# Attention output of two head pairs in the score tiles, fill steps behind AV, and two more GEMM blocks in the AV banks

## The chip, the cores and the metric

The kernel runs on one core of a Trainium2 chip. The metric is the device time of one execution in microseconds (us); smaller is better. The median of three runs of the kernel before is 334.15 us (333.97 to 334.6). Engines: PE multiplies matrices into PSUM, ACT does activations, DVE does vector work, POOL does elementwise work that doesn't touch PSUM, and SP issues DMAs.

## The reference, cut to what matters

```python
scores = scale * np.matmul(q, k.transpose(0, 1, 3, 2))     # 8 batches, 8 heads, 576 tokens, 64 wide
decay = cum[:, :, :, None] - cum[:, :, None, :]            # cum: running sum of log f
attn = softmax(np.where(causal, -1e9, scores + decay))
x = np.matmul(attn, v)                  # -> (4608 tokens, 512)
h = x @ w_in                            # 512 -> 2048
g = 0.5 * h * (1.0 + erf(h / sqrt(2)))  # gelu
out = g @ w_out                         # 2048 -> 512
```

The decay is put into the values: each key's row of V is multiplied by its weight, and a 65th column holds the weight itself, so that AV (attention weights times V) gives both the sum and its divisor.

## The kernel before, in words

The program goes through the eight batches one by one; the order of every engine's work is written out by hand, and each engine takes its instructions in that order. Heads are worked in four pairs, 0 to 3. Batches 0 and 1 have code of their own; `attention(b)` is for batches 2 to 7, and the change is in what it does for batches 3 to 7. Such a batch has two stages.

*Attention.* For each pair and each of four score tiles, `scores` (L299) multiplies K with Q into a score tile, ACT takes exp of it (L329), POOL masks the diagonal (L331). Between the score tiles PE does steps of the second GEMM of the batch before, taken from a generator (`take`, L590; `gemm2_rows`, L489). A step is one or two matmuls of 512 columns (L509); there are 64, in four groups of 16 by rows of tokens. 53 of them lie between score tiles (`FILL`). Then comes AV: `attend` (L343) does 15 matmuls of 65 columns for each head (L350), and `normalize` (L358) on DVE takes the reciprocal of five divisors (L363) and multiplies 128x320 values by them into `x` (L364). When both heads of a pair are done, `x_dma` (L388) has SP issue a transposing DMA of `x` into slice i of `xT`. Ten of the last eleven steps of the fill are put among the AV groups by `FILL_AV` (L826): none before pair 0, then three, two and two before pairs 1 to 3, and one between the two heads of each of these. A copy of a partial sum that was put off (L887) and the last step follow; that step's sum goes out by L533 and L537.

*First GEMM and gelu.* `gemm1` (L400) does blocks of 128 of the 2048 columns: four matmuls of 512 columns (L405), one for each contraction slice, and slice i is what pair i's transpose brings. `gemm1_open` (L829) opens seven blocks: all slice 0 of blocks 0 to 5, then all slice 1, and so on, so that later slices may come later. Blocks 0 to 3 lie in the two score tiles, 4 and 5 in the two AV banks, 6 in another bank. The other blocks (L981 on) follow one by one. ACT takes gelu of each (L425) and then its bank is free. Meanwhile DVE puts the next batch's Q and K in order (`untangle`, L269) and POOL weighs its V (`weigh_v`, L288).

PSUM has eight banks: `s_psum`, two score tiles of two banks each; `o_psum`, two single banks for AV; `m_psum`, two single banks for the GEMMs. A pool hands its buffers out in turn, and whoever writes one first waits until its last reader is through. Blocks 7 and 10 to 15 take `m_psum`; blocks 8 and 9 take `o_psum` (`spare`, L416), by the line

```python
aside = ffb in ((7, 8) if b == 2 else (8, 9)) if b > 1 else b == 1 and ffb % 4 < 2
```

After block 15 the next batch's attention begins, and the first two groups of its fill take `o_psum` and then `m_psum` (`PLAN`, L472). After batch 7 the second GEMM of batch 7 and both GEMMs of the 64 last tokens of all batches follow (L435).

Of the kernel before, what the change touches and what calls it, by code (L numbers as in the profile page):

```python
# [9 lines left out]
FP32 = mybir.dt.float32  # L10
BF16 = mybir.dt.bfloat16
Act = mybir.ActivationFunctionType
Alu = mybir.AluOpType
PSUM = bass.MemoryType.PSUM

P = 128
S = 576
D = 64
H = 8
HP = 4  # L20
NBLK = 5
# [20 lines left out]
def where(n, m):  # L42

    q = K0[m]
    for t, parts in enumerate(STILES):
        c = 0
        for nn, q0, w in parts:
            if nn == n and q0 <= q and q + P <= q0 + w:
                return t, c + q - q0
            c += w  # L50
    raise KeyError((n, m))
# [3 lines left out]
def kernel(  # L55
# [10 lines left out]
    nc = tc.nc  # L66
# [20 lines left out]
    x_pool = ctx.enter_context(tc.tile_pool(name="x", bufs=4))  # L87
# [3 lines left out]
    s_psum = ctx.enter_context(tc.tile_pool(name="s_psum", bufs=2, space=PSUM))  # L91
# [37 lines left out]
    def load_v(b, h0=0, h1=H, eng=nc.sync, ns=range(NBLK)):  # L129
        if b >= B:  # L130
            return
        for n in ns:
            p0 = D if n == NBLK - 1 else 0
            eng.dma_start(
                v_sb[p0:P, h0:h1, n, :],
                v[b, h0:h1, K0[n] + p0 : K0[n] + P].rearrange("h p d -> p h d"),
            )
# [203 lines left out]
    o_of, x_of, xT_of = {}, {}, {}  # L341

    def attend(b, i, h, ms, pool=o_psum, tag="o"):  # L343
        if (b, i, h) not in o_of:
            o_of[b, i, h] = pool.tile([P, NBLK, D + 1], FP32, tag=tag, name="o")
        o = o_of[b, i, h]
        for m in ms:
            for n in range(m + 1):
                t, c = where(n, m)
                nc.tensor.matmul(  # L350
                    o[:, m, :],
                    e_of[b, i, t][:, h, c : c + P],
                    vw_of[b][:, 2 * i + h, n, :],
                    start=(n == 0),
                    stop=(n == m),
                )

    def normalize(b, i, h):  # L358
        if (b, i) not in x_of:
            x_of[b, i] = x_pool.tile([P, NBLK, 2, D], BF16, tag="x", name="x")  # L360
        o = o_of[b, i, h]
        r = x_pool.tile([P, NBLK], FP32, tag="r", name="r")
        nc.vector.reciprocal(r, o[:, :, D])  # L363
        nc.vector.tensor_tensor(  # L364
            x_of[b, i][:, :, h, :],
            o[:, :, 0:D],
            r.unsqueeze(2).to_broadcast([P, NBLK, D]),
            Alu.mult,
        )

    def xT(b):
        if b not in xT_of:
            xT_of[b] = xT_pool.tile([P, n_dm, XC], BF16, tag="xT", name="xT")
        return xT_of[b]
# [13 lines left out]
    def x_dma(b, i):  # L388
        nc.sync.dma_start_transpose(
            xT(b)[:, i, :].rearrange("d (m p) -> d m p", p=P),  # L390
            x_of[b, i].rearrange("p m h d -> p (m h d)"),
        )

    def x_tail(b):
        nc.gpsimd.tensor_copy(tails[:, :, b * TL : (b + 1) * TL], xT(b)[:, :, XC - TL :])
# [20 lines left out]
    def spare():  # L416
        return o_psum.tile([P, TC], FP32, tag="o", name="ps1")
# [167 lines left out]
    def gemm2_third():  # L585
        yield from gemm2_second(0)
        yield from gemm2_rows(0, PLAN_0)
        yield from gemm2_rows(1, PLAN_1)

    def take(gen, n):  # L590
        for _ in range(n):
            if next(gen, "end") == "end":
                return
# [229 lines left out]


    FILL = [[8, 4, 3, 3], [3, 3, 3, 3], [3, 3, 3, 3], [3, 3, 3, 2]]
    FILL_AV = [(0, 0), (3, 1), (2, 1), (2, 1)]  # L826
    FILL_2 = [[8, 8, 8, 8], [8, 8, 4, 4], [4, 4, 4, 4], [4, 4, 4, 4]]

    def gemm1_open(b):  # L829


        pss = []
        for _ in range(2):
            wide = s_psum.tile([P, 2, 512], FP32, tag="s", name="ps1")
            pss += [wide[:, 0, :], wide[:, 1, :]]
        pss += [spare(), spare(), m_psum.tile([P, TC], FP32, tag="m", name="ps1")]
        for kt in range(2):
            for ffb in range(6):
                gemm1(b, ffb, (kt,), pss[ffb])
        gemm1(b, 6, (0, 1), pss[6])  # L840
        for ffb in range(7):
            gemm1(b, ffb, (2,), pss[ffb])
        for pair in ((4,), (5,), (6,), (0, 1), (2, 3)):
            for ffb in pair:
                gemm1(b, ffb, (3,), pss[ffb], False)
            for ffb in pair:
                gelu(b, ffb, pss[ffb])

    def attention(b):


        fill = gemm2_third() if b == 2 else gemm2_rows(b - 1, PLAN)
        counts = FILL_2 if b == 2 else FILL

        def av(i, n=0):
            for h in range(2):
                attend(b, i, h, (0, 1, 2, 3, 4))
                normalize(b, i, h)
                if h == 0:
                    take(fill, n)  # L860
            x_dma(b, i)

        for i in range(HP):
            for t in range(4):
                scores(b, i, t)
                take(fill, counts[i][t])
                if t == 1 and b == 2 and i > 0:
                    av(i - 1)
                    if i == 1:
                        load_v(3)  # L870
                if b == 2 and (i, t) == (0, 3):
                    weigh_v(b, 2)
                    weigh_v(b, 3)
                if b > 2 and i == 0 and t == 1:
                    load_v(b + 1)
                if b > 2 and t == 0 and i < 2:
                    transpose_dma(b + 1, 4 * i, 4 * i + 4)
                if b == 2 and t == 1 and i == 1:
                    transpose_dma(3, 0, 4)
        if b == 2:  # L880
            take(fill, 4)
            av(HP - 1)
        else:
            for i, (n0, n1) in enumerate(FILL_AV):
                take(fill, n0)
                av(i, n1)
            put_off.pop()()  # L887
        if b == 2:
            take(fill, 4)
            transpose_dma(3, 4, 8)  # L890
        take(fill, 999)

        if b == 2:
            pss = [gemm1(b, ffb, (0, 1)) for ffb in range(2)]
            pss += [spare(), spare()]
            for ffb in range(2):
                gemm1(b, ffb, (2,), pss[ffb])
            for ffb in (2, 3):
                gemm1(b, ffb, (0, 1, 2), pss[ffb])
            for ffb in range(4):  # L900
                gemm1(b, ffb, (3,), pss[ffb])
            more = s_psum.tile([P, 2, 512], FP32, tag="s", name="ps1")
            gemm1(b, 4, ps=more[:, 0, :])
        else:
            gemm1_open(b)
        if b + 1 < B:
            untangle(b + 1, 0)
            weigh_v(b + 1, 0)
        x_tail(b)
# [64 lines left out]
    for b in range(B):  # L974
        if b == 0:
            first_attention()
        elif b == 1:
            second_attention()
        else:
            attention(b)  # L980
        for ffb in range(4 if b < 2 else 5, n_ff):  # L981
            if b == 0 and ffb in HELD:
                continue
            aside = ffb in ((7, 8) if b == 2 else (8, 9)) if b > 1 else b == 1 and ffb % 4 < 2
            if b <= 2 or ffb > 6:
                gemm1(b, ffb, ps=spare() if aside else None)
            if b == 1 and ffb % 2 == 0:
                at = HELD[(ffb - 4) // 2]
                gelu(0, at, h_of[at])
            if b == 0:  # L990
                if ffb == 4:
                    attend_tail()
                if ffb == 5:
                    tail_0()
                if ffb == 7:
                    weigh_v(1, 0)
                    load_w_out(0)
                    weigh_v(1, 1)
                    load_w_out(1)
                    load_qk_tokens(2)  # L1000
                if ffb == 8:
                    transposes_first(1, 0, o_psum, "o")
            elif b + 1 < B:
                first, gap = (5, 3) if b == 1 else (1, 4)
                at, late = divmod(ffb - first, gap)
                if late == 0:
                    untangle(b + 1, at)
                if late == gap - 2 and (b > 1 or at < 2):
                    weigh_v(b + 1, at)
                if ffb == (9 if b == 1 else 14):  # L1010
                    load_qk_tokens(b + 2)
# [34 lines left out]
```

## Time and profile before

| what | value |
|---|---|
| median of three runs | 334.15 us |
| profiled execution | 335.06 us, its span 333.4 us |
| PE busy | 323.6 us, 97% of the span |
| ACT, DVE, POOL busy | 203.1, 189.1, 134.1 us |
| first GEMM, L405 (512 matmuls on `xT`) | 115.1 us busy, 1.7 us idle before them |
| AV, L350 (840 matmuls) | 33.9 us busy |
| division, L364 (56) and L363 (56) | 27.5 and 10.7 us busy, 491 and 192 ns each |
| transposes of `x`, issued by SP | 24, median 2.5 us from issue to landing, 4.8 at most |
| instruction queue's packets in the DMA records | 26 of 16 KB |

The profile is of one execution. The page gives each engine's busy time, the chain of work that ended last, and the costliest groups of instructions with what their engine waited for. The timeline gives start (us from the span's beginning), duration, engine, line, operation, output and input, count, and in brackets the idle time before it and what ended it. Consecutive matmuls overlap in it, because a matmul's row runs to the end of its pipeline: the time that one adds is the distance between starts. Batches 3 to 7 begin their AV at 126.8, 161.9, 197.2, 231.9 and 266.5 us and their first GEMM at 133.0, 168.1, 203.6, 238.2 and 272.7 us.

### The profile page before, as it was taken

How to read it: one execution, taken by the hardware profiler on the slowest of the kernel's cores; microseconds unless marked ns; L12 is line 12 of the kernel's file. 1: busy time of each engine (PE TensorE's matmuls, PEld its weight loads, DVE VectorE, ACT ScalarE, POOL GpSimd, SP SyncE). 2: the span in 40 equal slices, each digit the busy share in tenths (PEclk: the TensorE clock that was granted, in tenths of full speed). 3: DMA queues.
4: the chain of work that ended last, by engine and by line, in shares of the span. 5: the costliest groups of instructions: out<-in, count | busy, mean ns of one | idle time of the engine just before them, and what ended most of it. 6: DMA issues, size and time to landing. Idle time of an engine off the chain costs nothing.

```text
span 333.4 us, 8154 instructions
## 1 busy us (share of the span) xinstructions
PE 323.6 (97%) x3327; PEld 173.6 (52%) x3327; DVE 189.1 (57%) x432; ACT 203.1 (61%) x296; POOL 134.1 (40%) x260
## 2 busy tenths in 40 slices
PE   8999999999999999999999999999999999999995
PEld 4664455445544467445644565456645564444443
DVE  5852756754649637993599459964896370010011
ACT  4986786965526894389618980899078916405600
POOL 8997873057336152725345443535152500000000
PEclk9999999999999999999999999999999999999999
DMA  7999999959999697399978987779600151020022
GB/s 120 195 199 213 198 194 147 216 113 219 185 196 179 113 222 146 71 144 190 211 93 119 175 206 135 105 136 218 155 21 2 65 101 43 2 90 36 0 53 76
DMA packets 94949, 44.19 MB, mean 133 GB/s; under 512 B 74176, under 2 KB 89792, under 8 KB 94912
## 3 DMA queue, kind: packets, MB, share of 16 engines
q1 hardware_dynamic: 77760, 27.16, 40.7%
q0 software_dynamic: 16752, 15.99, 30.3%
q8 instruction: 26, 0.43, 0.6%
q10 hardware_dynamic: 400, 0.52, 0.4%
q14 instruction: 11, 0.09, 0.1%
HBM read 36.85 MB, written 9.44 MB: 139 GB/s over the span
## 4 chain that ended last, share of the span: by engine, by line
PE 82%; DMA 11%; POOL 5%; issue 1%; ACT 0%; DVE 0%; POOLq 0%
PE ps L405 33%; PE ps L509 26%; PE ps L449 8%; PE o L350 6%; PE s L319 6%; DMA xT<-x 5%; DMA q<-in_k_dram 3%; DMA k<-in_k_dram 3%; POOL v_sb L169 2%; PE ps L573 1%; POOL q L120 1%; PE ps L549 1%; POOL k L120 1%; POOL w_in_sb L184 1%; POOL vw L288 0%
## 5 line engine op out<-in xcount | busy, mean ns | idle before, releaser
L425 ACT ACTIVATE g<-ps 128x512 bf16<-128x512 f32 x138 | 75.8, 618 | 89.4 <-PE ps L405 88.3
L405 PE MATMUL ps<-xT,w_in_sb 128*128 128x512 bf16 x512 | 115.1, 379 | 1.7 <-DMA xT<-x 1.6
L509 PE MATMUL ps<-w_out_sb,g 64*128 64x512 bf16 (+1 forms) x751 | 111.2, 376 | 0.0
L329 ACT ACTIVATE e<-s 128x896 bf16<-128x896 f32 x112 | 87.8, 836 | 14.9 <-PE s L319 12.7
L405 PEld LDWEIGHTS <-w_in_sb 128*128 128x128 bf16 x576 | 55.2, 97 | 68.8 <-issue 6.2
L331 POOL TENSOR_SCALAR_AFFINE_SELECT e<-e 128x256 bf16<-128x256 bf16 (+1 forms) x135 | 49.1, 383 | 76.1 <-ACT e L329 75.7
L509 PEld LDWEIGHTS <-g 64*128 64x128 bf16 (+1 forms) x751 | 41.9, 94 | 27.4 <-issue 1.3
L288 POOL TENSOR_TENSOR vw<-v_sb,wT 128x640 bf16<-128x640 f32 (+1 forms) x30 | 38.2, 1276 | 38.0 <-PE o L350 23.0
L269 DVE COPY qT<-tq 64x288 bf16<-64x288 bf16 x96 | 41.8, 436 | 3.1 <-DMA tq<-q 1.6
L269 DVE COPY kT<-tk 64x288 bf16<-64x288 bf16 x96 | 40.7, 424 | 2.7 <-DMA tk<-k 1.1
L523 DVE COPY ot<-ps 128x512 f32<-128x512 f32 x20 | 13.8, 692 | 49.5 <-PE ps L509 49.5
L319 PE MATMUL s<-qT,kT 64*128 64x256 bf16 (+1 forms) x336 | 37.8, 275 | 0.8 <-DVE kT L241 0.6
L350 PEld LDWEIGHTS <-e 128*128 128x128 bf16 x840 | 31.5, 98 | 9.1 <-issue 6.1
L350 PE MATMUL o<-vw,e 128*128 128x65 bf16 x840 | 33.9, 194 | 0.0
L458 DVE COPY ot<-ps 128x512 f32<-128x512 f32 (+2 forms) x9 | 5.7, 632 | 49.2 <-PE ps L449 49.2
L364 DVE TENSOR_TENSOR x<-o,r 128x320 bf16<-128x320 f32 x56 | 27.5, 491 | 1.9
L319 PEld LDWEIGHTS <-kT 64*128 64x128 bf16 x336 | 18.1, 94 | 19.8 <-issue 3.5
L449 PE MATMUL ps<-w_out_sb,g 128*128 128x512 bf16 (+2 forms) x144 | 28.0, 355 | 0.0
L449 PEld LDWEIGHTS <-g 128*128 128x128 bf16 x144 | 13.5, 98 | 14.5
L533 DVE TENSOR_TENSOR ot<-ot,ps 128x512 f32<-128x512 f32 x27 | 18.6, 688 | 2.5
L363 DVE RECIPROCAL r<-o 128x5 f32<-128x5 f32 x56 | 10.7, 192 | 7.8 <-PE o L350 7.8
L405 PE MATMUL ps<-tails,w_in_sb 128*128 128x512 bf16 x64 | 14.3, 378 | 0.0
(90 smaller groups left out, 186.2 us busy)
## 6 DMA issues: line engine op xcount, KB each, us to landing
out_dram<-ot SPq DMA_DIRECT2D x32, 256.0 KB, 2.5
v_sb<-in_v_dram SPq DMA_DIRECT2D x24, 256.0 KB, 4.8
q<-in_q_dram POOLq DMA_DIRECT2D x6, 576.0 KB, 6.2
k<-in_k_dram POOLq DMA_DIRECT2D x6, 576.0 KB, 8.4
v_sb<-in_v_dram POOLq DMA_DIRECT2D x17, 128.0 KB, 6.1
w_in_sb<-in_moe_w_in_dram POOLq DMA_DIRECT2D x4, 512.0 KB, 8.2
w_out_sb<-in_moe_w_out_dram POOLq DMA_DIRECT2D x4, 512.0 KB, 7.6
v_sb<-in_v_dram SPq DMA_DIRECT2D x6, 128.0 KB, 4.5
```

The costliest lines, as they stand in the source:

```text
L269: nc.vector.tensor_copy(rows[:, odd], src[odd * D : (odd + 1) * D, 2 * i + h].rearrange("d j p -> d p j"),)
L288: eng.tensor_tensor(vw(b)[:, hs, n0:n1, 0:D], v_sb[:, hs, n0:n1, :], w.unsqueeze(3).to_broadcast([P, 2, n1 - n0, D]), Alu.mult,)
L319: nc.tensor.matmul(to, *ab, start=half < 0, stop=half == 1 or not masked)
L329: nc.scalar.activation(et[:, :, z:c], st[:, :, z:c], Act.Exp, scale=scale)
L331: nc.gpsimd.affine_select(out=et[:, :, c0 + z : c0 + P], in_=et[:, :, c0 + z : c0 + P], compare_op=Alu.is_ge, fill=0.0, base=z, pattern=[[ ...
L350: nc.tensor.matmul(o[:, m, :], e_of[b, i, t][:, h, c : c + P], vw_of[b][:, 2 * i + h, n, :], start=(n == 0), stop=(n == m),)
L364: nc.vector.tensor_tensor(x_of[b, i][:, :, h, :], o[:, :, 0:D], r.unsqueeze(2).to_broadcast([P, NBLK, D]), Alu.mult,)
L405: nc.tensor.matmul(ps, w_in_sb[:, kt, ffb * P : (ffb + 1) * P], src[:, kt, 0:TC], start=(kt == 0), stop=(kt == n_dm - 1),)
L425: nc.scalar.activation(g_of[c][ffb], ps, Act.Gelu)
L449: nc.tensor.matmul(pss[ts][:, c0:c1], g_of[c][kt][:, ts * P : (ts + 1) * P], w_out_sb[:, kt, c0:c1], start=(kt == 0), stop=(kt == n_ff - 1),)
L509: nc.tensor.matmul(banks[r], g_of[c][kt][rows, ts * P : (ts + 1) * P], w_out_sb[rows, kt, :], start=kt == (steps.index("r") if r else 0), ...
L533: nc.vector.tensor_tensor(ot, ot, bank, Alu.add)
```

## The change

In batches 3 to 7 the AV of pairs 1 and 2 goes into two score tiles, one bank for each head, in place of the AV banks; each of these pairs is divided by one reciprocal of 10 divisors and one multiplication of 128x640 values for both heads. Pairs 0 and 3 stay in the AV banks with a division for each head. All eleven last steps of the fill come behind the AV of all pairs. In the first GEMM blocks 12 and 13 take the AV banks too.

```diff
-    FILL_AV = [(0, 0), (3, 1), (2, 1), (2, 1)]
...
+    def av_both(b, i):
+        st = s_psum.tile([P, 2, 512], FP32, tag="s", name="o2")
+        both = st[:, :, 0 : NBLK * (D + 1)].rearrange("p h (m d) -> p h m d", m=NBLK)
+        for h in range(2):
+            o_of[b, i, h] = both[:, h]
+            attend(b, i, h, (0, 1, 2, 3, 4))
+        x_of[b, i] = x_pool.tile([P, NBLK, 2, D], BF16, tag="x", name="x")
+        r = x_pool.tile([P, 2, NBLK], FP32, tag="r2", name="r2")
+        nc.vector.reciprocal(r, both[:, :, :, D])
+        nc.vector.tensor_tensor(
+            x_of[b, i].rearrange("p m h d -> p h m d"),
+            both[:, :, :, 0:D],
+            r.unsqueeze(3).to_broadcast([P, 2, NBLK, D]),
+            Alu.mult,
+        )
+        x_dma(b, i)
...
         else:
-            for i, (n0, n1) in enumerate(FILL_AV):
-                take(fill, n0)
-                av(i, n1)
+            av(0)
+            av_both(b, 1)
+            av_both(b, 2)
+            av(3)
             put_off.pop()()
...
-            aside = ffb in ((7, 8) if b == 2 else (8, 9)) if b > 1 else b == 1 and ffb % 4 < 2
+            aside = ffb in ((7, 8) if b == 2 else (8, 9, 12, 13)) if b > 1 else b == 1 and ffb % 4 < 2
```

In the changed kernel the wide reciprocal is L838, the wide multiplication L839 and the put-off copy L906.

## The prediction

> **What bounds the kernel now.** I read the page first. TensorE is busy for 97% of the span, every slice grants it full clock, and by the page's chain of waits most of the span is PE work. The change leaves PE's instructions as they are, so all it can win is PE time lost inside batches 3 to 7. The view of waits gives the sum that PE's own row admits to:
>
> ```profile
> PE 323.6 (97%) x3327; PEld 173.6 (52%) x3327; DVE 189.1 (57%) x432; ACT 203.1 (61%) x296; POOL 134.1 (40%) x260
> ...
> q8 instruction: 26, 0.43, 0.6%
> ```
> ```profile
> PE ps L405 <- DMA xT<-x: 1.6, 3, 0.6
> ```
>
> Three waits, 1.6 us, all of the first GEMM (L405) for transposed attention output. A modelled matmul end hides part of a wait, so I take distances between starts. The timeline of PE in batch 4, from the first pair's AV on (start, duration, engine, line, operation, tiles, count):
>
> ```profile
> 161.94 1.13 PE L350 MATMUL o<-vw,e 128*128 128x65 bf16 x30
> 162.90 0.81 PE L509 MATMUL ps<-w_out_sb,g 128*128 128x512 bf16 x3
> 163.55 0.64 PE L350 MATMUL o<-vw,e 128*128 128x65 bf16 x15
> ...
> 167.91 0.38 PE L509 MATMUL ps<-w_out_sb,g 128*128 128x512 bf16 x1
> 168.12 3.18 PE L405 MATMUL ps<-xT,w_in_sb 128*128 128x512 bf16 x14
> 171.87 4.48 PE L405 MATMUL ps<-xT,w_in_sb 128*128 128x512 bf16 x20 [0.56 <-DMA xT<-x]
> ```
>
> Three fill steps last from 162.90 to 163.55: 0.2155 us each. Fourteen GEMM matmuls at that pace from 168.12 end at 171.14; the next starts at 171.87: 0.73 us lost, at contraction slice 2, which is pair 2. The same reading in batches 3, 5 and 7:
>
> ```profile
> 132.99 1.46 PE L405 MATMUL ps<-xT,w_in_sb 128*128 128x512 bf16 x6
> 134.88 2.32 PE L405 MATMUL ps<-xT,w_in_sb 128*128 128x512 bf16 x10 [0.44 <-DMA xT<-x]
> ```
> ```profile
> 203.16 0.38 PE L509 MATMUL ps<-w_out_sb,g 128*128 128x512 bf16 x1
> 203.61 6.64 PE L405 MATMUL ps<-xT,w_in_sb 128*128 128x512 bf16 x30
> ```
> ```profile
> 272.68 1.46 PE L405 MATMUL ps<-xT,w_in_sb 128*128 128x512 bf16 x6
> 274.70 3.61 PE L405 MATMUL ps<-xT,w_in_sb 128*128 128x512 bf16 x16 [0.56 <-DMA xT<-x]
> ```
>
> Batch 3: due 132.99 + 6 x 0.2155 = 134.28, came 134.88: 0.60 (pair 1). Batch 5: due 203.375, came 203.61: 0.24 (pair 0). Batch 7: due 273.97, came 274.70: 0.73 (pair 1). Batch 6 loses nothing. Together **2.30 us**. A second loss stands on the weight row, in a short stretch of batch 4:
>
> ```profile
> 178.10 1.90 ACT L425 ACTIVATE g<-ps 128x512 bf16<-128x512 f32 x3
> ...
> 179.34 0.74 PEld L405 LDWEIGHTS <-w_in_sb 128*128 128x128 bf16 x4 [0.25 <-issue]
> ```
>
> Sixteen matmuls (four blocks) remain at 179.34, so it stands at block 12, which takes the bank of block 10, while ACT is still at that block's gelu. The trace has 351 ns instead of 213 between the two matmul starts there, once in each of the five batches: 5 x 0.138 = **0.69 us**.
>
> **Why transposes land late.** The transposes' issue-to-landing times by single issues: 2.4 us where undisturbed, but in each batch one of the four took longest: 4.1 (batch 3, pair 1), 4.6 (4, pair 2), 4.3 (5, pair 0), 3.1 (6, pair 1), 4.4 (7, pair 1); the one behind it took up to 3.7. In each case a 16 KB packet of the instruction queue falls into the flight. The DMA view for 167.20 to 168.48, pair 2 of batch 4:
>
> ```profile
> q8 instruction: 1, 0.02, 8.7%
> ...
> xT<-x SPq DMA_TRANSPOSE x1, 4.6
> ```
>
> The packet records put it at 168.46 for 1.78 us, and 23 of the transpose's packets, normally 18 ns, then take about 2 us. The Trainium skill (Runtime: NRT & Kernel Launch, Instruction fetch mechanics) says that crossing a 16 KiB block of instructions costs a queue bump, "mostly hidden". For PE itself the trace agrees; for DMAs in flight it does not, by the 4.6 us above. By the page the late landings would have another cause, an earlier issue would clear them all, and the time would be 331.2; by the rows it is the sum below.
>
> **The change part by part.** Per batch 3 to 7:
>
> *Order on PE.* 120 AV matmuls (8 heads of 15) with 10 of 11 fill steps among them become 120 in a row and 11 steps behind them (one was there already). From 163.55 to 168.12 six runs of AV and eight steps take 4.57 us; 6 x 0.474 + 8 x 0.2155 = 4.57, so changing between them costs nothing now, and putting them in two blocks gains or costs nothing on PE: 0. The first GEMM starts at the same place, 4.09 us after pair 0's transpose is issued (164.03 to 168.12).
>
> *The new banks.* Pair 1 goes into the score tile of the last pair's third step, pair 2 into that of its fourth. Their exps end at or before 162.41 (ACT's row in the same timeline), their AV would start at 162.9 and 163.85: no wait. Pair 3 needs the two AV banks of pair 0, divided by 163.34 and 163.97, at 164.8: no wait. The GEMM's first four blocks take the score tiles at 168.12, divided by about 166.3. The score-tile cover is 1.9 us; if it were gone, block 2 would wait for the second division.
>
> *Division.* Four small pieces (195 + 491 ns each) become two wide ones. The trace has no 128x640 division; below, one 128x320 row (0.49), above, two of them (0.98). The rows 128x320 at 491 and the addition of 128x512 at 688 (L533) give 1.03 ns an element, so 0.82; I take that, nearest to L533. With a reciprocal of 0.2 a pair needs 1.03 us.
>
> *Transposes.* Now x of pairs 0 to 3 is ready at
>
> ```profile
> 163.48 0.49 DVE L364 TENSOR_TENSOR x<-o,r 128x320 bf16<-128x320 f32 x1
> ...
> 165.14 0.49 DVE L364 TENSOR_TENSOR x<-o,r 128x320 bf16<-128x320 f32 x1
> ...
> 166.74 0.49 DVE L364 TENSOR_TENSOR x<-o,r 128x320 bf16<-128x320 f32 x1
> ...
> 168.34 0.49 DVE L364 TENSOR_TENSOR x<-o,r 128x320 bf16<-128x320 f32 x1
> ```
>
> and issues follow at 164.03, 165.66, 167.26, 168.85. After: AV of pair 1 is through at 163.85 (plus 0.2), DVE is free at 163.97, so ready at 165.0, 166.1 and, by two small divisions more, 167.5. SP's queue holds each transpose about 1.25 us, so issues come at 164.03, 165.3, 166.55 and 167.8: **0, 0.36, 0.7 and 1.05 us earlier**. SP's next store, the put-off copy (0.68) and the last sum behind it on DVE come earlier as well. Weighting the next batch's V on POOL, which waits for the last AV, starts 2 us earlier, beside divisions: L364 took 491 to 493 ns in all 56 cases, POOL's L288 beside some of them, so 0.
>
> *What waits remain.* With t the issue of pair 0, slices 0 to 3 are needed at t + 4.1, 5.4, 7.1 and 8.6. Undisturbed, transposes land at t + 2.4, 3.7, 4.95 and 6.2: no wait. The one that meets the instruction packet lands 3.1 to 4.6 after its issue: pair 0 is then up to 0.5 late, pair 1 (t + 4.4 to 5.9) up to 0.5, pairs 2 (7.1) and 3 (8.4) not. The packet goes with PE's place in its instructions; AV ahead of the fill brings those places of the AV phase about 1 us earlier, and I cannot say which pair it meets. One meeting a batch, the four pairs alike: (0.2 + 0.2 + 0 + 0) / 4 = 0.1, times five 0.5 us; bounds 0 and 5 x 0.5 = 2.5.
>
> *Blocks 12 and 13.* They follow blocks 8 and 9 in the AV banks, whose gelus are done over 1 us before; blocks 14 and 15 then follow 10 and 11, ready at 179.3 and 180.0, needed at 180.9 and 181.8. The 0.138 goes. The next batch's second GEMM takes the AV banks behind them: gelu 13 ends at 181.9, its first L509 starts at 183.1: 1.2 us of cover, 0.
>
> **Sum.** -2.30 + 0.5 - 0.69 = -2.49 us. The profiled execution took 335.06 (span 333.4 and 1.66 around it): 332.6 for such a one. It lies 0.9 above the median; taken off 334.15, **331.7**.
>
> **Rivals.**
> *A: waits stay, moved.* The packet meets pair 0 or 1 in nearly every batch. For it: the AV phase moves toward these pairs' flights, and pair 0 gains no lead. Against: 2.5 is the worst in all five. With waits as before only 0.69 is won: 333.5.
> *B: slower, PE is issue-bound.* 120 AV matmuls with their loads in a row outrun PE's sequencer, where fill steps gave it 0.2 us each to run ahead. It decides above 15.8 ns an instruction (31.7 ns a matmul and load); at 20 ns it costs 240 x 4.2 ns = 1.0 a batch, 5.0 in all: with the gains 336.7. Against: runs of 30 AV keep 31.7 ns; 36 transposes with loads (L226) took 0.48 us, 6.7 ns an instruction.
> *C: slower, wide division.* Above about 2.07 us each, block 2 waits for pair 2's score tile; at 2.4 it costs 2 x 0.33 x 5 = 3.3, less 0.69: 336.8 with today's waits. Against: the rows' upper end is 0.98.
> The program does what the change says: the order of instructions shows AV, then fill, and both wide divisions in all five batches.
>
> **How the numbers follow.** Forecast 0.82, A 0.12, B and C 0.06. Forecast: 331.2 with no wait left, 332.7 with 0.3 a batch; A reaches 333.5, so the range is 331.0 to 333.5. About 0.2% (0.67 us) is what a measurement of this kernel can tell from no change: faster below 333.48, all of the forecast and half of A: 0.88; same 0.07; slower 0.05.
>
> **What would show it.** Right: L405 waits for xT under 0.7 us in all, at slices 0 or 1 only; L839 near 0.82 us; transposes about 1.25 us apart; no gap at block 12; AV at 31.7 ns throughout. Wrong: AV runs spaced above 32 ns (B), L839 above 2 us (C), landings over 5 us after issue or waits at slice 2 (A, or a cause I have not seen).

## The result and the profile after

The changed kernel takes 332.6 us (median of 22 runs) where the kernel before takes 334.73 (22 runs): ratio 0.9943, 95% interval 0.992 to 0.9966, so 1.9 us less (1.1 to 2.7). Comparisons leave out runs that the chip disturbed. The profiled execution took 332.24 us, its span 330.5. PE's row and the instruction queue's on the page, and the view of waits:

```profile
PE 322.2 (97%) x3327; PEld 173.0 (52%) x3327; DVE 184.6 (56%) x412; ACT 203.0 (61%) x296; POOL 134.5 (41%) x260
...
q8 instruction: 26, 0.43, 0.6%
```
```profile
PE ps L405 <- DMA xT<-x: 0.6, 1, 0.6
```

Three waits have become one. The span fell by 2.9 us, but 0.7 of that lies ahead of the change: batch 3's AV now begins at 126.08, in the profile before at 126.81. From there to the end it is 204.42 us, before 206.55: 2.13 us less. Batch 3 on PE's timeline, which holds the one wait:

```profile
126.08 3.98 PE L350 MATMUL o<-vw,e 128*128 128x65 bf16 x120
129.90 2.54 PE L509 MATMUL ps<-w_out_sb,g 128*128 128x512 bf16 x11
133.04 13.33 PE L405 MATMUL ps<-xT,w_in_sb 128*128 128x512 bf16 x61 [0.61 <-DMA xT<-x]
```

120 AV matmuls start within 3.82 us, 31.8 ns each as before; 11 steps end at 132.27; the GEMM comes at 133.04: 0.77 us lost, now at slice 0. Batch 4 loses nothing:

```profile
165.07 2.54 PE L509 MATMUL ps<-w_out_sb,g 128*128 128x512 bf16 x11
167.45 4.91 PE L405 MATMUL ps<-xT,w_in_sb 128*128 128x512 bf16 x22
```

Batches 5 to 7 neither. The weight loads of batch 4's last blocks, broken at block 12 before, now run through:

```profile
176.08 4.85 PEld L405 LDWEIGHTS <-w_in_sb 128*128 128x128 bf16 x23
181.35 0.11 PEld L319 LDWEIGHTS <-kT 64*128 64x128 bf16 x4 [0.42 <-issue]
```

The divisions of batch 4 on DVE's timeline:

```profile
162.80 0.49 DVE L364 TENSOR_TENSOR x<-o,r 128x320 bf16<-128x320 f32 x1
163.37 0.22 DVE L838 RECIPROCAL r<-o 128x10 f32<-128x10 f32 x1
163.63 0.82 DVE L839 TENSOR_TENSOR x<-o,r 128x640 bf16<-128x640 f32 x1
164.37 0.21 DVE L838 RECIPROCAL r<-o 128x10 f32<-128x10 f32 x1
164.62 0.82 DVE L839 TENSOR_TENSOR x<-o,r 128x640 bf16<-128x640 f32 x1
```

The wide multiplication takes 823 to 825 ns in all ten cases. The Trainium skill (VectorE: DVE Perf Modes, The TRN2 errata) has (N + 151) / 0.96 ns for an fp32 addition of two tensors; an estimate by it for 640 is 824. The trace agrees for this multiplication.

### The profile page after: what moved, and what is told of

Its sections match the earlier page's. It is cut to its first block, busy times and chain, and to the rows that moved or that the text cites. A ratio compares the mean times of both kernels' runs of the same rounds, so it can differ in the third digit from the quotient of the medians.

```text
span 330.5 us, 8129 instructions
## 1 busy us (share of the span) xinstructions
PE 322.2 (97%) x3327; PEld 173.0 (52%) x3327; DVE 184.6 (56%) x412; ACT 203.0 (61%) x296; POOL 134.5 (41%) x260
## 4 chain that ended last, share of the span: by engine, by line
PE 94%; ACT 2%; DMA 1%; DVE 1%; issue 1%; SPq 0%; DVEq 0%
PE ps L405 38%; PE ps L509 27%; PE ps L449 8%; PE o L350 8%; PE s L319 6%; DMA xT<-x 1%; PE s L623 1%; PE ps_w L210 1%; ACT e L628 1%; PE ps_f L226 1%; PE ps L573 1%; PE ps L549 1%; PE o L654 1%; ACT e L329 0%; PE ps_x L383 0%
## 5 line engine op out<-in xcount | busy, mean ns | idle before, releaser
L509 PE MATMUL ps<-w_out_sb,g 64*128 64x512 bf16 (+1 forms) x751 | 106.3, 376 | 0.0
L509 PEld LDWEIGHTS <-g 64*128 64x128 bf16 (+1 forms) x751 | 42.6, 94 | 32.2 <-issue 1.3
L269 DVE COPY qT<-tq 64x288 bf16<-64x288 bf16 x96 | 44.1, 459 | 3.5 <-DMA tq<-q 2.0
L269 DVE COPY kT<-tk 64x288 bf16<-64x288 bf16 x96 | 38.3, 399 | 2.7 <-DMA tk<-k 1.1
L350 PEld LDWEIGHTS <-e 128*128 128x128 bf16 x840 | 27.9, 98 | 4.3 <-issue 2.4
L350 PE MATMUL o<-vw,e 128*128 128x65 bf16 x840 | 29.0, 194 | 0.0
L533 DVE TENSOR_TENSOR ot<-ot,ps 128x512 f32<-128x512 f32 x27 | 18.6, 688 | 4.1 <-PE ps L509 1.8
L364 DVE TENSOR_TENSOR x<-o,r 128x320 bf16<-128x320 f32 x36 | 17.7, 492 | 1.2
L395 POOL COPY tails<-xT 128x256 bf16<-128x256 bf16 x7 | 3.4, 486 | 29.1 <-DMA xT<-x 27.2
```

The source lines that it names most:

```text
L269: nc.vector.tensor_copy(rows[:, odd], src[odd * D : (odd + 1) * D, 2 * i + h].rearrange("d j p -> d p j"),)
L350: nc.tensor.matmul(o[:, m, :], e_of[b, i, t][:, h, c : c + P], vw_of[b][:, 2 * i + h, n, :], start=(n == 0), stop=(n == m),)
L364: nc.vector.tensor_tensor(x_of[b, i][:, :, h, :], o[:, :, 0:D], r.unsqueeze(2).to_broadcast([P, NBLK, D]), Alu.mult,)
L509: nc.tensor.matmul(banks[r], g_of[c][kt][rows, ts * P : (ts + 1) * P], w_out_sb[rows, kt, :], start=kt == (steps.index("r") if r else 0), ...
L533: nc.vector.tensor_tensor(ot, ot, bank, Alu.add)
```

## What the experiments were to tell apart

My theory: two separate losses were taken away. PE waited for transposes that a packet of its own instruction queue had delayed, and block 12 waited for a bank. Rivals: the order alone, the wide division alone or the two blocks alone make the gain; or the lateness belongs to the stage (when x is ready, the stores) and not to the packet.

I read four numbers from each trace: the time from batch 3's first AV to the end ("stage"), the waits for transposes and the gaps at block 12 (both as distances between starts, less 0.2155 us a matmul; distances of two matmuls, which come from missing records, are left out), and what is left.

| kernel | stage | waits | gaps | rest |
|---|---|---|---|---|
| before | 206.55 | 2.29 | 0.68 | 203.58 |
| before, again (e8) | 206.48 | 2.18 | 0.67 | 203.63 |
| changed | 204.42 | 0.77 | 0 | 203.65 |
| changed, again (e9) | 204.66 | 1.01 | 0 | 203.65 |
| blocks alone (e1) | 204.93 | 1.32 | 0 | 203.61 |
| blocks alone, again (e12) | 205.09 | 1.42 | 0 | 203.67 |
| AV alone (e2) | 204.39 | 0.06 | 0.67 | 203.66 |
| narrow division (e4) | 203.83 | 0.16 | 0 | 203.67 |
| changed, 64 instructions on (e5) | 204.08 | 0.40 | 0 | 203.68 |
| changed, 128 on (e6) | 203.81 | 0.14 | 0 | 203.67 |
| before, 128 on (e7) | 204.64 | 0.35 | 0.67 | 203.62 |
| changed, 104 on, wide warm-up cut (e10) | 204.02 | 0.38 | 0 | 203.64 |

The rest is 203.58 to 203.68 in twelve executions of nine programs: nothing else that the change does costs or gains more than about 0.1 us, neither 40 divisions made into 30 nor the moved fill.

## One part of the change at a time

**e1_blocks**, the blocks alone:

```diff
-  ... else (8, 9)) if b > 1
+  ... else (8, 9, 12, 13)) if b > 1
```

> The kernel before with blocks 12 and 13 alone in the AV banks. Theory (two separate gains: transposes that land late, and block 12's wait for its bank): the 351 ns distance at block 12 becomes about 213 in all five batches, -0.69 us in all; the waits for transposes stay as in the kernel before, about 2.3 us by starts. About 333.5 to 334.1 where the kernel before has 334.2 to 334.7. Rival (the gain is one chain, and only AV earlier frees the blocks): the gap stays or goes to block 14.

Measured: 333.27 us, ratio 0.9949 (0.9927 to 0.9971). No gap at block 12 or 14 in any batch, as expected; but the gain, 1.7 us by the ratio, is larger than the gaps' 0.68 that I had expected, since the waits are 1.32 us and not 2.3. Batch 7 waits for nothing: its pair 1 lands 2.4 us after its issue, 4.4 before.

**e12_blocks_again**, the same program:

> Blocks 12 and 13 alone once more, for a second profile. Its first had waits for transposes of 1.3 us where the kernel before has 2.2 and 2.3 in two profiles, because batch 7's pair 1 landed in time. If that was luck of one execution, the waits are now 2.0 to 2.4 us and batch 7 waits again about 0.7; if the earlier end of each first GEMM (0.14 us a batch) moves the packets against the transposes for good, they are again 1.2 to 1.5 us with none in batch 7. No gap at block 12 in either.

Measured: 337.69 us in one execution (334.2 for the kernel before beside it). It came to batch 3 4.8 us later than e1's profile of the same program, so only the stage is read: waits 1.42 us, again none in batch 7. So this is no luck of one execution: a program whose stages end 0.14 us earlier meets other delays. How so small a shift spares pair 1 there I did not find out. It lands at t + 4.0 (t is pair 0's issue) in both, and a packet of the instruction queue starts at t + 3.9; in two profiles of the kernel before one starts at t + 4.1 and 3.6, and pair 1 lands at t + 6.1 and 6.0. So the start of a packet by the records does not alone say which transpose it delays.

**e2_av**, the changed kernel with blocks 12 and 13 back in the other banks:

> The changed kernel with blocks 12 and 13 back in the other banks. Theory: the 0.138 us at block 12 is there again in each batch (0.69 in all), waits for transposes stay small as in the changed kernel (one of about 0.77 us); about 1.5 us under the kernel before. Rival (blocks 12 and 13 make the gain): as slow as the kernel before.

Measured: 333.2 us, ratio 0.995 (0.9916 to 0.9984). The gap at block 12 is back in each batch (0.67 us); the waits are 0.06 us, where I had expected about 0.77. By time neither half can be told from the whole: either has about 1.7 us, together they have 1.9. So the rivals "blocks alone" and "AV alone" do not fall by time; what tells them apart is the trace, where the blocks take the gaps away and AV does not, and AV takes away more of the waits. The gains don't add up, because each edit also moves the waits: 0.06 us here, 0.77 and 1.01 with the blocks besides.

**e3_av_banks**, the order without the score tiles:

```diff
-  av_both(b, 1)
-  av_both(b, 2)
+  av(1)
+  av(2)
```

> The changed kernel's order (all AV, then all eleven steps), but pairs 1 and 2 in the two AV banks, divided head by head as before. Theory: each head from the third on waits until DVE has divided the head two before it, 0.70 us a head against 0.474 of AV: eight heads take about 5.4 us in place of 3.8, 1.6 us a batch on PE, 8 us in all; no wait for transposes remains. Net about 5 to 6 us slower than the kernel before: the score tiles are what carries the order. Rival (the order by itself makes the gain): as fast as the changed kernel.

Measured: 341.26 us, ratio 1.0192 (1.0164 to 1.022), 6.4 us slower. Batch 4 on PE's timeline:

```profile
164.70 1.13 PE L350 MATMUL o<-vw,e 128*128 128x65 bf16 x30
166.25 1.18 PE L350 MATMUL o<-vw,e 128*128 128x65 bf16 x30 [0.43 <-DVE r L363]
167.79 1.19 PE L350 MATMUL o<-vw,e 128*128 128x65 bf16 x30 [0.36 <-DVE r L363]
169.33 1.19 PE L350 MATMUL o<-vw,e 128*128 128x65 bf16 x30 [0.35 <-DVE r L363]
170.57 2.32 PE L509 MATMUL ps<-w_out_sb,g 128*128 128x512 bf16 x10
```

Each pair waits for the division of the pair before: pair 1 starts at 166.25, when DVE has divided the first head of pair 0 (at 166.10) and is at the second. From AV to GEMM it is 8.03 us in place of 6.19, 9.2 in five batches, and no wait for transposes is left: 203.65 + 9.2 = 212.85 against a measured stage of 212.86. The fill among the AV groups had covered the division; the score tiles are what lets it go.

**e4_narrow**, pairs 1 and 2 in the score tiles, divided head by head:

```diff
-  nc.vector.reciprocal(r, both[:, :, :, D])
-  nc.vector.tensor_tensor(...)      # 128x640
+  for h in range(2):
+      normalize(b, i, h)
```

> The changed kernel with pairs 1 and 2 in the score tiles, but divided head by head (two reciprocals of 5 and two multiplications of 128x320 each). Theory: the pairs' x is ready 0.1 to 0.7 us later (0.70 a head in place of 1.05 a pair, and DVE can start one head earlier), transposes still 0.2 to 1 us ahead of the kernel before; within 0.5 us of the changed kernel. Rival (the wide division and the shorter DVE time make the gain): about 1.5 us slower than the changed kernel.

Measured: 332.12 us, ratio 0.9918 (0.9892 to 0.9944); waits 0.16 us. By time it can't be told from the changed kernel (the intervals overlap); its stage is 0.6 and 0.8 us shorter than the two of the changed kernel, all of it in the waits. The wide division is not where the gain comes from.

## The instruction packet

If the packets go by PE's place in its program, more PE instructions at the start move them against the stages and change nothing else there.

```diff
   warm_up(9)
+  warm_up(32, D)     # e5, on the changed kernel; e6: 64; e7: 64, on the kernel before
```

**e5_shift32**

> The changed kernel with 32 more small matmuls (64 columns, with their loads: 64 PE instructions) in the warm-up at the start; nothing else. Theory (the late landings come from the packets of PE's instruction queue, which go by PE's place in its program): in the AV phase the packet comes about 1 us earlier against pair 0's issue t: batch 3 from t + 1.2 to t + 0.2, batch 5 from + 0.7 to - 0.3, batch 6 from + 1.3 to + 0.3, batch 7 from + 1.8 to + 0.8, batch 4 from + 3.7 to between + 1.3 and + 2.2. The 0.77 us wait of batch 3 goes; batch 4 may get one of up to 0.7. Rival (the stores or something else fixed to the stage delays pair 0): pair 0 is late in the same batches as in the changed kernel, and batch 3 keeps its wait.

**e6_shift64**

> The changed kernel with 64 more small matmuls (128 PE instructions) in the warm-up. Theory (instruction packets): packets come about 2 us earlier than in the changed kernel, ahead of pair 0's issue in batches 3, 5, 6 and 7, and at t + 0.3 to + 1.2 in batch 4; pair 0 lands about 2.4 us after its issue in batches 3, 5, 6 and 7; waits of L405 for transposes 0.2 us or less in all. Rival (fixed to the stage): as in the changed kernel, 0.77 us in batch 3.

**e7_before64**

> The kernel before with the same 64 small matmuls in the warm-up. Theory (instruction packets): packets come about 3 us earlier against pair 0's issue t than in the kernel before (there t + 3.7, + 4.4, + 1.2, + 2.3 and + 4.1 in batches 3 to 7), so that pairs 1 and 2 are no longer hit; L405's waits for transposes fall from 2.30 us to at most 0.8, pair 0 of batch 4 being the one still at risk; the gap at block 12 stays. Rival (the waits come from how late x is ready): they stay at about 2.3 us, in batches 3, 4 and 7.

When the packet started, against pair 0's issue t (by the packet records; two where two lay near):

| batch | changed | e5 | e6 | before | e7 |
|---|---|---|---|---|---|
| 3 | +1.2 | +0.2 | +0.4 | +3.7 | +0.3 |
| 4 | -1.6, +3.7 | +1.8 | +0.4 | -1.2, +4.4 | +2.3 |
| 5 | +0.7 | -1.5, +4.5 | +1.8 | +1.2 | +3.8 |
| 6 | +1.3 | 0.0 | -1.6, +3.8 | +2.3 | -1.2, +4.3 |
| 7 | +1.8 | +0.6 | -0.4 | +4.1 | +0.6 |

The packets moved, and the late pairs with them. In e5 four of five came within 0.3 us of where I had put them; batch 3's wait is gone, and the one left (0.40) is pair 2 of batch 5, in whose flight the next packet falls. There SP's stores ahead of pair 0 also took 2.22 us in place of 1.39, beside the packet at t - 1.5, and all four transposes were issued 0.5 us late. In e6 batches 3 and 5 were not clear of them as I had expected, yet the waits are 0.14 us in all. e7 decides: the order and the times at which x is ready are those of the kernel before, and its waits fall from 2.29 to 0.35 (pair 2 of batch 6; the pair that I had thought at risk, pair 0 of batch 4, was not). Batch 4 of e7, which waits for nothing, where the kernel before lost 0.73:

```profile
169.84 0.38 PE L509 MATMUL ps<-w_out_sb,g 128*128 128x512 bf16 x1
170.05 2.32 PE L405 MATMUL ps<-xT,w_in_sb 128*128 128x512 bf16 x10
```

So lateness belongs to the packet, and the rival "fixed to the stage" falls. It also means that 128 idle PE instructions give batches 3 to 7 about as much as the change does (stage 204.64 against 204.42 and 204.66 for the whole change, 204.39 for AV alone). An earlier issue is worth something besides: in batch 6 a packet meets pair 2 in e6 as in e7, and it lands at t + 7.21 in e6 after a flight of 4.60 us, at t + 7.42 in e7 after one of 4.19; the waits are 0.14 and 0.35. By total times e5, e6 and e7 show no gain that can be told (332.97, 336.23 and 335.68 in one execution each, 334.05 before). They pay for the matmuls at the start: the warm-up's row on PE is 1.05, 2.04 and 2.79 us longer. Batch 3 begins 1.1, 4.6 and 2.5 us later than without them; what else came into these single executions is open, since e1 and e12, one program, differ by 4.8 there.

What the packet does to a flight, in the DMA view for 128.2 to 129.5 of the changed kernel (batch 3, pair 0):

```profile
q8 instruction: 1, 0.02, 6.6%
...
xT<-x SPq DMA_TRANSPOSE x1, 4.6
```

The packet moves 16 KB from 129.46 on for 1.36 us; from 129.90 on, 18 of the transpose's 256-byte packets are in flight for 1.54 to 1.70 us in place of 18 ns, and the transpose lands 4.6 us after its issue in place of 2.4. The Trainium skill (DMA: Bandwidth & Descriptors, Queues, rings and completion order) says that each DMA engine goes round its queues and serves a whole packet before it turns to the next queue. That fits 18 packets held for about as long as the 16 KB take; that they are those of one engine, the runs do not show.

**e8_before_again**

> The kernel before once more, unchanged, for a second profile of its batches 3 to 7. If the waits go by PE's place alone, they are within 0.3 us of the first profile's 2.29 us, in the same batches. If a packet's own duration (0.94 to 1.78 us in the profiles so far) and a lag of a tenth of a microsecond decide, they are anywhere from 1.3 to 2.5 us, since transposes that landed just in time in one profile miss in the next. The gap at block 12 is 0.69 us in both.

Measured: 335.01 us in one execution; waits 2.18 us, in the same batches and 0.2 in batch 6 besides.

**e9_after_again**

> The changed kernel once more, unchanged, for a second profile. The instruction packet meets pair 0 again in batches 3, 5, 6 and 7 (0.7 to 1.8 us after its issue) and pair 2 in batch 4; pair 0 has 4.1 us, so that only a flight above that waits: between 0 and 0.8 us in all; no gap at block 12.

Measured: 332.96 us in one execution; waits 1.01 us, more than the 0.8 expected at most, all in batch 3 (flight 4.87 us, packet 1.54 us long); pair 0 is met in batches 3, 5, 6 and 7 and pair 2 in batch 4, as in the first profile. In these pairs of profiles the place of the waits is the program's; the one wait of the changed kernel was longer where the packet took longer (1.54 us against 1.36).

## Two attempts to get the rest

**e10_shift_free**

```diff
-  warm_up(9)
+  warm_up(1)
+  warm_up(60, D)
```

> The changed kernel, its nine warm-up matmuls of 512 columns replaced by one of them and 60 of 64 columns (104 PE instructions more, in about the same time). Theory (instruction packets): packets at about t + 0.8 in batches 3 and 4, + 2.2 in 5, + 4.1 in 6, before t in 7; waits for transposes 0 to 0.4 us in all, so at most 0.8 us under the changed kernel, which these rounds can hardly tell; slower by what the start loses if 60 small matmuls take longer than eight wide ones (64 of them took 2.1 us more at the start of an earlier run).

Measured: 334.88 us, ratio 1.0003 (0.9969 to 1.0036). Its profile has 0.38 us of waits, as expected, and a stage of 204.02 (packets at t + 0.8 and 1.8 in batches 4 and 5, but at t - 0.1 to t in 3, 6 and 7, where I had put only that of 7 so early); yet by time the gain is gone. The profiled execution (333.01) is the fastest of its twelve; where the others lose about 2 us no trace shows, and it stays open.

**e11_more_behind**

```diff
-  [3, 3, 3, 2]]
+  [3, 3, 2, 1]]
...
   av(3)
+  take(fill, 2)
   put_off.pop()()
```

> The changed kernel with two more fill steps taken from between the last pair's score tiles and put behind the AV (13 there in place of 11, the first two of them pairs of half-height matmuls). Pair 0 has about 4.5 us in place of 4.1: a flight of 4.6 costs 0.1 in place of 0.5 to 0.8, so waits for transposes 0 to 0.3 us. Against it, PE has 0.43 us less beside the last exps: if ACT paces that stretch, PE waits for the score tile up to 0.43 us a batch, 2.2 us in all. Theory (fill behind AV is worth no more than the wait it covers): within 0.8 us of the changed kernel.

Measured: 333.89 us, ratio 0.9986 (0.9954 to 1.0019): most of the gain is lost, though no wait for transposes is left. Batch 4 on PE's timeline (this execution reached batch 3 over 4 us late; only the stages behind are read):

```profile
165.74 4.14 PE L350 MATMUL o<-vw,e 128*128 128x65 bf16 x120
169.81 0.61 PE L509 MATMUL ps<-w_out_sb,g 64*128 64x512 bf16 x4
170.58 2.32 PE L509 MATMUL ps<-w_out_sb,g 128*128 128x512 bf16 x10 [0.16 <-DMA xT<-x]
```

Between AV and GEMM there are 6.99 us in place of 6.19. Two steps are 0.43. They are half-height matmuls, and each change between half and full height costs 0.096 us (127 and 309 ns between starts in place of 31 and 213); one before AV was there already, two more come behind it. And AV itself waits 0.16 us at its second head, 0.05 us behind the end of DVE's addition L533 (166.34), presumably the reader of that bank, with two steps less in front of it. (The 0.16 in the last row is no wait for a transpose: a record is missing there, and the distance is 534 or 535 ns in all five batches, whenever pair 0 lands.) 0.8 a batch makes 4.0; 5 x 0.43 is saved between the scores; of the 2.3 us by which the stage is longer than the common rest, that leaves 0.5 I have not traced. Theory and bound failed here: I had priced the move by ACT's pace alone.

## Why the prediction was right, and where it was off

The forecast was 2.49 us less, 331.7 from 334.15, with 331.0 to 333.5 as the range; measured are 332.6 from 334.73, 1.9 us less by the runs (1.1 to 2.7), 2.13 and 1.82 by the stages of two profiles each.

- *Blocks 12 and 13: -0.69.* Right: the 351 ns at block 12 are gone in all five batches and nothing took their place (rest unchanged; e1). The matmuls around it are 215 to 216 ns apart and not 213, so that it was 0.68.
- *Order on PE, new banks: 0.* Right: 31.8 ns a matmul over runs of 120, no wait for a score tile. e3 shows what the banks are worth.
- *Division: 0.82 us, chosen between 0.49 and 0.98.* Right (0.824). It mattered less than I made it: e4 does without.
- *Transposes earlier by 0, 0.36, 0.7 and 1.05.* Right in batch 4 alone: issues at t, t + 1.29, 2.61 and 3.93 (forecast 1.27, 2.52 and 3.77; the kernel before 1.62, 3.23 and 4.82). Without a packet they land after 2.4 us. In the other four batches SP too was held beside the packet, which the forecast left out: one transpose of each batch has a row of 1.88 to 2.10 us on SP in place of 1.20 to 1.23, and pairs 2 and 3 are issued at t + 3.41 to 3.69 and 4.73 to 5.01. Against the kernel before, the lead of pairs 2 and 3 was 0.3 us at most there.
- *Waits left: 0.5.* Too small: 0.77 and 1.01. The step that was mis-sized is "one meeting a batch, the four pairs alike". In both profiles the packet met pair 0 in four batches of five: AV ahead of the fill had moved it there, which I had noted and not worked out. Three of these flights of 3.4 to 3.9 us still fit into 4.1. The sign of a right forecast, waits under 0.7 us, was missed. And a flight can be longer than my bound of 4.6: it was 4.87 behind a packet of 1.54 us. The wait is longer, too, than the flight's excess: in batch 3 pair 0 landed at 132.91 and the GEMM began at 133.04, where batch 5 of the kernel before, at pair 0 too, took 0.04 from landing to matmul. There the weights had been loaded at 203.17, ahead of the landing; now the first weight load comes behind it, at 133.01.
- *Luck.* The forecast had the waits fall because transposes gain lead. Batch 4 shows that: pair 2 flew 4.22 us, landed at t + 6.83 and was needed at t + 7.1; issued at t + 3.23 as before, it would have been 0.35 late. In the other batches the packet fell on pair 0, which gains no lead, and that three of its flights just fitted is luck: with the same AV order e2 lost 0.06 us and the changed kernel 0.77 and 1.01, and e7 brings the kernel before to 0.35 by moving alone. So the sum came out near, but for most of the waits not by the step that it was argued from.
- *Rivals.* A came true in part: the waits moved to pair 0, but only one batch pays. B and C did not come: no run of AV was spaced above 32 ns on average, and the wide division was far from 2.07 us. The Trainium skill's rule (Runtime: NRT & Kernel Launch, Instruction fetch mechanics) that such a fetch is mostly hidden would have given 331.2; for DMAs in flight the runs differ, by 0.77 and 1.01 us of waits left and by e7.

## What to carry to other kernels

When a transfer lands late now and then, look for what else the DMA engines carry at that moment before you blame the code that issues it; a long unrolled program fetches its own instructions through them. Such waits hang on where the stage lies in the program, so that two edits that each remove them don't add up, and a gain of half a per cent can come from moving and not from mending: shift the program by some idle instructions and see whether the gain stays. Work that covers a wait of one engine may cover another's as well: before it is moved, see what the freed engine will wait for next, here the banks that the division held.

## What the runs showed of the hardware that I had not expected

- 16 KB instruction packets took 0.9 to 1.85 us beside transposes, and a transpose they met landed up to 4.9 us after its issue in place of 2.4.
- Where they fall is the program's: in two profiles of each of three programs the waits lay in the same batches but for one of 0.2 us, and their sums within 0.3 us of each other.
- Beside such a packet SP's own row of a transpose, 1.20 to 1.23 us undisturbed, was up to 2.1 us long at pair 0 or 1 of the changed kernel (2.45 at pair 3 of batch 4 of the kernel before), so that the transposes behind it were issued later.
- A change between half-height and full-height matmuls cost 0.096 us on PE each time.
